# New orders for a fused DeltaNet and Fourier-mix kernel: a plan in which loads in flight delay instruction packets

## The chip, the cores and the metric

The kernel runs on one core of a Trainium2 chip. Its time is the device time of one execution in microseconds (us); the median of the runs is compared. Engines are named as in the profile: PE is TensorE's matrix multiply and PEld its weight load, DVE is VectorE, ACT is ScalarE, POOL is GpSimd, SP is the engine that issues most loads and stores.

## The reference

Two blocks stand one behind the other, all in 32-bit floats. The first is a DeltaNet recurrence over 768 positions for 4 batches of 8 heads with 48 channels; the second mixes positions and channels by a Fourier transform, normalises each row, and applies a two-layer MLP.

```python
for t in range(S):
    y[:, :, t] = np.einsum('bhd,bhde->bhe', q[:, :, t], state)
    v_old = np.einsum('bhde,bhd->bhe', state, kt)
    state = state + bt[:, :, :, None] * np.einsum('bhd,bhe->bhde', kt, vt - v_old)
...
X = np.fft.fft(x, axis=1)                      # x is y as (batch, position, 384)
X = np.fft.fft(X, axis=2)
u = x + np.real(X)
un = (u - mean(u)) / np.sqrt(var(u) + 1e-06)
out = u + np.maximum(un @ w_ch1, 0.0) @ w_ch2   # 384 -> 1536 -> 384
```

`kt` is `k` divided by its norm, `bt` the factor beta.

## The kernel before

The recurrence is done in chunks. A unit is 128 positions of one batch with all 8 heads; there are 24 units, six for each batch. For each unit the kernel loads keys, queries and values, turns keys and queries with transposes on TensorE (`turn`), forms products of keys with keys and of queries with keys (`keys`, `gram`), and inverts a triangular matrix of 32x32 blocks for all its heads. The inversion is a long chain of small products and sums on VectorE. Units are inverted in rounds: four and two units for batch 0 (`begin16`, `invert16` in blocks of 16, put together by `join` with matmuls of `gd` and `w2` or `w1`), then three units for each round (`begin`, `invert`). After that the state runs through the units one half (64 positions) at a time: `chain0`, `values0` and `outputs0` for batch 0, `step` and `outputs` for the others. The tiles `us0` to `us5` hold a unit's keys, queries and values; a later unit takes the tile of an earlier one when that is done.

When a batch is complete, `mixing` does its second block: `folds` uses the symmetries of the Fourier transform on VectorE, `seq` multiplies by the table `tab` along positions, `half_axis` copies the result out of PSUM (`g0`) and mirrors it (`g2`), `feat` multiplies by `ft` along channels, `normed` normalises and transposes, and `mlp` or `mlpw` does the MLP. The MLP's matmuls are the bulk of TensorE's time; those of one batch fill TensorE while VectorE inverts for the next. The weights are loaded in pieces and recoded at the start by ScalarE, VectorE and GpSimd (`weights`), with stages in tiles that are used for something else later (`ws`, `x1`, `R0`, `R1`).

Nothing of the order is written out by hand. Each operation is recorded by `Plan.op` with its engines and estimated durations, what it reads and writes, its PSUM banks and a priority. `Plan.schedule` then runs through an imitated time: each engine takes, when it is free, the ready operation with the least `pr`, which comes from the due times, the priority and a small pseudo-random shift (`shift`, by `KEYS`, one key for each 64 operations). The instructions are given out in that order, and on the chip each engine works through its own list in order and waits by semaphores for data alone: the imitated times are not on the chip.

The plan imitates several things of the chip. `speed` imitates TensorE's clock by its load in windows of `WIN` us, at half speed when cold. `fetch` imitates the packets in which TensorE's instructions come, one for each `BLOCK` of 256 instructions; an operation can't end before its packet has come. `bursts` are the stretches in which loads are in flight; with `HOLDUP` at 0.0, they delay no packet before the change. `moved` is the time at which the loads so far have landed, at `RATE` KB per us.

Where TensorE has nothing to do and its load would fall below a target, the plan puts in a filler (`idle`): matmuls on `pb` or `pack` into a free bank, whose result nobody reads. A filler is six matmuls of 64 columns in the first 5 us of the plan, later one of 256 columns on 128 rows or two on 64 rows each. The opening, from the first load to the first matmul of `join`, thus consists of transposes and products of keys with fillers between them.

Two small things are also touched. `half` holds the 1e-6 under the roots: `pads` zeroes it, then `eps` sets it on GpSimd; the first square root on ScalarE reads it, and a load of ScalarE's function table comes with that. Two long memsets of `w2` and `w1` and one of `bcol` stand on GpSimd at the start as well. And in `half_axis`, `g0` copies a PSUM row that holds the positions in `m` groups into one in which they alternate.

Of the kernel before, what the change touches and what calls it, by code (L numbers as in the profile page):

```python
# [21 lines left out]
KEYS = [0, 0, 850, 0, 0, 0, 0, 0, 0, 0, 0, 0, 582, 124, 156, 527, 24, 416, 593, 575, 248, 102, 531, 777, 887, 940, 929, 917, 359, 0, 859, 298, 364, 930, 55, 217, 906, 105, 134, 603, 98, 513, 101, 281, 683, 240, 529, 252]  # L22
# [10 lines left out]
class Op:  # L33
# [4 lines left out]
RATE = 190.0  # L38
WIN, WARM, COLD, CLOCK = 3.413, 600.0, 560.0, True
LOOK, EARLY = 1e9, 19.0271  # L40
FOLD, BY, SEQ, HOT, HOTPE, HOTPK, HOTG, NORM = 1, 1, 1, 4.4058, 0, 0, 0, 1
HOTC, PORT, E2 = 2, 1, 5.0
GAP, HALF = 0.2407, 77.3251
LATE = 2.2375
PLOOK, PHOLD, PEND = 32.7105, 0.4568, 120.0484
NHALF = 1
FORCE = 612.9049
BLOCK, LEAD, SEEK, LAND, LAND2, HOLDUP = 256, 60, 1.0, 2.4, 2.0082, 0.0
# [8 lines left out]
M00 = 90.055  # L57
M0, MP, MX, MN, MA, MT, MD = 89.6079, 112.2722, 14.7505, 25.9652, 19.5299, 4.5034, 5.8147


LATER = {"SHARE": 0.3855, "HOLD": 0.1688, "GAP2": 0.3021, "WAIT": 10.3631, "GATHER": 2.1078, "URGENT": -9.2156,
         "FIRST": 59.6475, "EV": 2.2994, "STAY": 0.4162, "CHAIN": 1.0}
START = {"SHARE": -0.1525, "HOLD": 0.3422, "GAP2": 0.0341, "WAIT": 8.3074, "GATHER": 1.5733, "URGENT": -10.6776,
         "FIRST": -0.9418, "EV": 10.7255, "STAY": 0.0, "CHAIN": 0.0}
LIM2 = {"state": 1, "sum": 4, "attn": 7, "mix": 5, "mlp": 6, "norm": 7, "win": 6}
# [6 lines left out]
class Plan:  # L72
# [114 lines left out]
    def schedule(self, pick, limits, switch, idle=None, span=()):  # L187
# [18 lines left out]
        moved, landed = 0.0, [0.0] * 8  # L206
# [12 lines left out]
        while done < n:  # L219
# [4 lines left out]
            for e in self.ENG:  # L224
# [3 lines left out]
                cand = [o for o in avail[e] if o.ready[e] <= now + 1e-9]  # L228
                if e != "PE":
# [72 lines left out]
                o = best  # L302
# [11 lines left out]
                if o.kb:  # L314
# [3 lines left out]
                    self.bursts.append((moved - o.kb / RATE + 1.0, moved + 0.7))  # L318
                    self.bursts = self.bursts[-6:]
# [34 lines left out]
            if not progressed:  # L354
# [3 lines left out]
                nxt += [s for s in slots if s is not None and s > now + 1e-9]  # L358
                nxt += [b.busy for e in ("DVE", "ACT") for o in avail[e] for b in o.banks
# [75 lines left out]
def kernel(  # L435
# [135 lines left out]
    def psum(b):  # L571
        return pst[b.slot]
# [951 lines left out]
    def half_axis(bk, gs, m, sn, pr):  # L1524
# [503 lines left out]
    P.op({"POOL": 0.3}, eps, [], [A(half, 0, 1)], -60, lat=LP)  # L2028
# [240 lines left out]
```

## Time and profile before

| | before |
|---|---|
| median of 3 runs | 646.76 us (646.76 to 652.67) |
| the profiled execution | 651.29 us, span 649.5 us |
| TensorE busy | 627.6 us (97%) |
| VectorE busy | 512.0 us (79%) |
| ScalarE busy | 268.3 us (41%) |
| GpSimd busy | 35.4 us (5%) |
| bytes moved | 32.01 MB, mean 49 GB/s |

The span goes from the first to the last instruction of the profiled execution; the rest of its time lies around it. A group of instructions is given by the line of the kernel that issues it. Helpers issue most of them: 533 is every matmul (`mm`), 536 every transpose on TensorE (`tr`), 542 a copy on ScalarE, 544 and 546 a copy on VectorE (`copy`), 580 a load (`dma`), 2224 and 2231 the fillers. A matmul shows as two records. The granted clock is the share of TensorE's full clock that the chip let through.

### The profile page before, as it was taken

To read this page: it belongs to the slowest core of one execution; us is meant where nothing else is said; L and a number is where in the kernel's file an instruction comes from. 1 tells how busy PE (TensorE), PEld (TensorE's weight loads), DVE (VectorE), ACT (ScalarE), POOL (GpSimd) and SP (SyncE) were. 2 spreads that over 40 slices of the span, in tenths; PEclk is the share of its full clock that TensorE was granted. 3 is DMA by queue.
4 is the path that set the end of the run, shared out by engine and by line. 5 is a ranking of instruction groups with operands and counts; after the bars stand their busy time and mean duration, and the time that the engine had idled before them with its cause. 6 is when DMAs were issued, how large, how long until landed. Compare 5 with 4: busy or idle time off the path is not lost.

```text
span 649.5 us, 23061 instructions
## 1 busy us (share of the span) xinstructions
PE 627.6 (97%) x9958; PEld 517.9 (80%) x9958; DVE 512.0 (79%) x1533; ACT 268.3 (41%) x784; POOL 35.4 (5%) x40
## 2 busy tenths in 40 slices
PE   8898989999999999999999999999999999999998
PEld 7698878876767777877777877777777789999997
DVE  5979959999996469999973899999838724986573
ACT  4768554652126544521645551435452113321120
POOL 3001212221000000000000000000000000000000
PEclk9989979999999999999999999999999999999999
DMA  9912456430003312000232310000000000000000
GB/s 189 283 76 45 97 124 150 110 106 2 24 3 88 77 40 51 25 2 1 52 63 53 65 50 2 1 26 3 4 28 3 1 25 1 26 1 25 2 25 24
DMA packets 82810, 32.01 MB, mean 49 GB/s; under 512 B 75667, under 2 KB 79732, under 8 KB 82580
## 3 DMA queue, kind: packets, MB, share of 16 engines
q1 hardware_dynamic: 82516, 30.31, 19.0%
q8 instruction: 78, 1.28, 0.8%
q10 hardware_dynamic: 192, 0.23, 0.1%
q14 instruction: 24, 0.20, 0.1%
HBM read 25.81 MB, written 4.72 MB: 47 GB/s over the span
## 4 chain that ended last, share of the span: by engine, by line
PE 75%; DVE 18%; issue 3%; ACT 3%; DMA 1%; SPq 0%; DVEq 0%; ACTq 0%
PE pp L533 70%; PE pp L2231 3%; PE pp L536 2%; DVE rr L1018 2%; DVE tmp L1013 2%; DVE R L1418 1%; DVE pm L1596 1%; DMA ws<-in_moe_w_ch_dram 1%; PE pp L2224 1%; ACT us L542 1%; DVE w L2001 1%; ACT R L542 1%; DVE x L1578 1%; DVE rr L820 1%; DVE us L782 1%
## 5 line engine op out<-in xcount | busy, mean ns | idle before, releaser
L533 PE MATMUL pp<-R,w 128*128 128x256 f32 (+1 forms) x832 | 182.2, 367 | 0.5 <-DVE x L1393 0.3
L533 PEld LDWEIGHTS pp<-R,w 128*128 128x128 f32 x832 | 145.9, 190 | 20.2 <-DVE x L1393 0.5
L533 PE MATMUL pp<-w,R 128*128 128x384 f32 x384 | 136.4, 499 | 0.9 <-DVE w L2001 0.9
L533 PEld LDWEIGHTS pp<-w,R 128*128 128x128 f32 x384 | 71.1, 192 | 43.2 <-issue 2.0
L542 ACT ACTIVATE us<-pp 32x128 f32<-32x128 f32 (+3 forms) x232 | 73.0, 349 | 72.0 <-PE pp L533 51.7
L533 PE MATMUL pp<-us 64*64 64x64 f32 (+4 forms) x2784 | 67.7, 230 | 7.1 <-issue 5.6
L1662 ACT ACTIVATE R<-pp 128x512 f32<-128x512 f32 x48 | 28.6, 596 | 98.5 <-PE pp L533 93.8
L533 PEld LDWEIGHTS pp<-us 64*64 64x64 f32 (+2 forms) x2784 | 57.1, 133 | 13.0 <-issue 9.1
L1018 DVE TENSOR_TENSOR rr<-rr,tmp 128x30 f32<-128x30 f32 (+14 forms) x180 | 55.7, 330 | 0.8
L1013 DVE TENSOR_TENSOR tmp<-rr 128x30 f32<-128x30 f32 (+14 forms) x180 | 55.0, 326 | 0.8
L533 PEld LDWEIGHTS pp<-u,us 64*64 64x64 f32 (+1 forms) x1472 | 36.9, 132 | 16.4 <-issue 10.4
L533 PE MATMUL pp<-u,us 64*48 64x48 f32 (+2 forms) x1472 | 43.2, 220 | 1.9 <-DVE u L544 0.7
L1327 DVE TENSOR_TENSOR u<-u,pp 64x192 f32<-64x192 f32 x66 | 21.9, 350 | 19.8 <-PE pp L533 17.1
L542 ACT ACTIVATE R<-pp 128x192 f32<-128x192 f32 (+7 forms) x76 | 25.0, 384 | 28.0 <-PE pp L536 14.1
L1837 DVE TENSOR_TENSOR us<-us,pp 128x256 f32<-128x256 f32 x64 | 26.8, 419 | 12.0 <-ACT us L542 10.2
L542 ACT ACTIVATE x<-pp 64x192 f32<-64x192 f32 (+1 forms) x80 | 24.4, 323 | 25.3 <-PE pp L533 22.6
L1356 DVE TENSOR_TENSOR st<-st,pp 128x192 f32<-128x192 f32 x30 | 10.5, 351 | 28.3 <-PE pp L533 28.2
L1793 DVE TENSOR_TENSOR gd<-us 128x128 f32<-128x128 f32 x48 | 11.9, 287 | 24.2 <-ACT us L1869 17.0
L542 ACT ACTIVATE u<-pp 64x192 f32<-64x192 f32 (+1 forms) x71 | 23.0, 326 | 17.9 <-PE pp L533 13.6
L2231 PE MATMUL pp<-pack 64*64 64x256 f32 (+1 forms) x170 | 29.0, 408 | 0.4 <-ACT R L542 0.4
L533 PE MATMUL pp<-st,us 48*64 48x48 f32 (+1 forms) x1232 | 27.9, 223 | 1.2 <-ACT us L542 0.9
L533 PEld LDWEIGHTS pp<-st,us 48*64 48x64 f32 x1232 | 23.8, 136 | 5.3 <-issue 3.7
(172 smaller groups left out, 997.0 us busy)
## 6 DMA issues: line engine op xcount, KB each, us to landing
out_dram<-x SPq DMA_DIRECT2D x11, 384.0 KB
us<-in_k_dram SPq DMA_DIRECT2D x16, 192.0 KB
us<-in_q_dram SPq DMA_DIRECT2D x16, 192.0 KB
us<-in_v_dram SPq DMA_DIRECT2D x16, 192.0 KB
us<-in_v_dram SPq DMA_DIRECT2D x8, 181.5 KB
us<-in_q_dram SPq DMA_DIRECT2D x8, 181.5 KB
us<-in_k_dram SPq DMA_DIRECT2D x8, 181.5 KB
x<-in_moe_w_ch_dram SPq DMA_DIRECT2D x3, 484.0 KB
```

The lines of the kernel that those rows point to most:

```text
L533: I(nc.tensor.matmul(o, lhsT=lhsT, rhs=rhs, start=start, stop=stop, skip_group_check=True))
L536: I(nc.tensor.matmul(o, lhsT=src, rhs=ident[p0:p0 + n, p0:p0 + n], is_transpose=True, start=start, stop=True, skip_group_check=True))
L542: I(nc.scalar.activation(o, i, ACT.Copy, **({} if scale is None else {"scale": scale})))
L782: I(eng(e).tensor_tensor(z.V, z.V, ro.nr(160 + 8 * ul, 8)[:, :, None].broadcast_to([128, H, D]), op=ALU.mult))
L1013: I(eng(e).tensor_tensor(T_, R[:, :, j + 1:32, j:j + 1].broadcast_to([128, ns, n, j]), R[:, :, j:j + 1, 0:j].broadcast_to([128, ns, n, j]) ...
L1018: I(eng(e).tensor_tensor(R[:, :, j + 1:32, 0:j], R[:, :, j + 1:32, 0:j], T_, op=ALU.add))
L1327: I(nc.vector.tensor_tensor(U[:, s], U[:, s], psum(b1[s])[a, s0:s1].rearrange("p (j d) -> p j d", d=D), op=ALU.subtract))
L1356: I(nc.vector.tensor_tensor(sn[:, s0:s1], so[:, s0:s1], psum(b2)[:, s0:s1], op=ALU.add))
L1662: I(nc.scalar.activation(o, s, ACT.Relu))
L1793: vec(128, lambda e, j=j, i0=i0, i1=i1, op=op: I(nc.vector.tensor_tensor(s(j), i0, i1, op=op)), [aH] + rd, [aS(j)], pr - P.ev)
L1837: vec(256, lambda e: I(nc.vector.tensor_tensor(o, i0(), i1(), op=ALU.add)), [], [aH] + list(wr), pr - P.ev, use=n)
L2231: I(nc.tensor.matmul(pst[two[0]][x, 0:256], lhsT=w[x, 0:n], rhs=w[x, 0:256], start=True, stop=True, skip_group_check=True))
```

## The change

The change has three kinds of edits.

First, the plan imitates more. `crowd` gives the share of the stretch from 0.5 us before to 1.5 us after a time in which loads are in flight, and `fetch` delays a packet by `HOLDUP`, now 1.8 us, times that share. The list of bursts is longer, and each ends 0.3 us later. `moved` begins at `MOVED`, 1.6 us, instead of 0, so that all loads land later in the plan. Between `PACE` and `PEND` of imitated time, SP gets no load until the loads before have moved (`PGAP`).

Second, nearly all constants of the plan and a good half of the `KEYS` are new, so the order of all engines is new from the first operations on.

Third, two operations are edited: `eps` has the priority -460 instead of -60, and `g0` runs through its row in the order of the destination, where it ran in the order of the source.

```diff
-KEYS = [0, 0, 850, 0, 0, 0, 0, 0, 0, 0, 0, 0, 582, 124, ...]
+KEYS = [555, 372, 229, 658, 0, 352, 821, 0, 0, 291, 803, 38, 709, 968, ...]
...
-LATE = 2.2375
-PLOOK, PHOLD, PEND = 32.7105, 0.4568, 120.0484
+LATE = -8.0806
+PLOOK, PHOLD, PEND = 28.9494, 0.7158, 110.1635
 NHALF = 1
-FORCE = 612.9049
-BLOCK, LEAD, SEEK, LAND, LAND2, HOLDUP = 256, 60, 1.0, 2.4, 2.0082, 0.0
+FORCE = 613.4279
+BLOCK, LEAD, SEEK, LAND, LAND2, HOLDUP = 256, 60, 1.0, 2.401, 1.9048, 1.8
+PACE, PGAP, MOVED = 4.1415, -0.0594, 1.6
...
-TARGET, SPANW = 688.3225, 2.1272
-E0, E1, D1 = 1.0, 10.0, 128.0771
-TSW = 114.3489
-LIM = {"state": 1, "sum": 3, "attn": 7, "mix": 4, "mlp": 5, "norm": 2, "win": 4}
-NW, IV, IV1, WP = 9, 13.8489, 26.4887, -10.2966
+TARGET, SPANW = 685.5687, 2.0943
+E0, E1, D1 = 1.0, 10.0, 105.9979
+TSW = 108.6907
+LIM = {"state": 1, "sum": 3, "attn": 7, "mix": 6, "mlp": 8, "norm": 2, "win": 4}
+NW, IV, IV1, WP = 9, 14.9091, 10.2325, -10.5791
...
+    def crowd(self, t):
+
+        return min(1.0, sum(max(0.0, min(z, t + 1.5) - max(a, t - 0.5)) for a, z in self.bursts) / 2.0)
...
-            for a, z in self.bursts:
-                if a <= t < z:
-                    t = min(z, t + HOLDUP)
-                    break
+            t += HOLDUP * self.crowd(t)
...
-        moved, landed = 0.0, [0.0] * 8
+        moved, landed = MOVED, [0.0] * 8
...
+                if e == "SP" and PACE < now < PEND:
+                    cand = [o for o in cand if not o.kb or moved + PGAP <= now + 1e-9]
...
-                    self.bursts.append((moved - o.kb / RATE + 1.0, moved + 0.7))
-                    self.bursts = self.bursts[-6:]
+                    self.bursts.append((moved - o.kb / RATE + 1.0, moved + 1.0))
+                    self.bursts = self.bursts[-12:]
...
-                o = Fv[0:n, g, 0:hs].rearrange("p (k a) -> p a k", a=m)
-                copy(e, o, psum(bk[g % 2])[0:n, 0:m * w].rearrange("p (a k) -> p a k",
-                                                                   a=m)[:, :, 0:w - 1])
+                o = Fv[0:n, g, 0:hs].rearrange("p (k a) -> p k a", a=m)
+                copy(e, o, psum(bk[g % 2])[0:n, 0:m * w].rearrange("p (a k) -> p k a",
+                                                                   a=m)[:, 0:w - 1])
...
-    P.op({"POOL": 0.3}, eps, [], [A(half, 0, 1)], -60, lat=LP)
+    P.op({"POOL": 0.3}, eps, [], [A(half, 0, 1)], -460, lat=LP)
```

More of the change, by code (lines that the diff above doesn't have):

```diff
@@ L40 @@
 LOOK, EARLY = 1e9, 19.0271
-FOLD, BY, SEQ, HOT, HOTPE, HOTPK, HOTG, NORM = 1, 1, 1, 4.4058, 0, 0, 0, 1
-HOTC, PORT, E2 = 2, 1, 5.0
-GAP, HALF = 0.2407, 77.3251
-LATE = 2.2375
-PLOOK, PHOLD, PEND = 32.7105, 0.4568, 120.0484
+FOLD, BY, SEQ, HOT, HOTPE, HOTPK, HOTG, NORM = 1, 1, 1, 2.0724, 0, 0, 0, 1
+HOTC, PORT, E2 = 1, 1, 5.0
+GAP, HALF = 0.3228, 84.1105
+LATE = -8.0806
+PLOOK, PHOLD, PEND = 28.9494, 0.7158, 110.1635
 NHALF = 1
-FORCE = 612.9049
-BLOCK, LEAD, SEEK, LAND, LAND2, HOLDUP = 256, 60, 1.0, 2.4, 2.0082, 0.0
+FORCE = 613.4279
+BLOCK, LEAD, SEEK, LAND, LAND2, HOLDUP = 256, 60, 1.0, 2.401, 1.9048, 1.8
+PACE, PGAP, MOVED = 4.1415, -0.0594, 1.6
 CUT, ROW = 512, 121
@@ L51 @@
 WF = 2, 2
-TARGET, SPANW = 688.3225, 2.1272
-E0, E1, D1 = 1.0, 10.0, 128.0771
-TSW = 114.3489
-LIM = {"state": 1, "sum": 3, "attn": 7, "mix": 4, "mlp": 5, "norm": 2, "win": 4}
-NW, IV, IV1, WP = 9, 13.8489, 26.4887, -10.2966
[L57 to L65, printed above, removed]
+TARGET, SPANW = 685.5687, 2.0943
[3 more added lines that the diff above has]
+NW, IV, IV1, WP = 9, 14.9091, 10.2325, -10.5791
+M00 = 102.6459
+M0, MP, MX, MN, MA, MT, MD = 89.6079, 112.293, 14.26, 39.3785, 20.7101, 5.6373, 6.1497
+LATER = {"SHARE": 0.3909, "HOLD": 0.1688, "GAP2": 0.3179, "WAIT": 10.0453, "GATHER": 2.2916, "URGENT": -9.2156,
+         "FIRST": 60.1548, "EV": -0.0518, "STAY": 0.4103, "CHAIN": 1.0}
+START = {"SHARE": -0.1569, "HOLD": 0.3422, "GAP2": 0.1697, "WAIT": 5.8104, "GATHER": 1.3282, "URGENT": -10.6776,
+         "FIRST": 2.0404, "EV": 10.4613, "STAY": 0.0, "CHAIN": 0.0}
+LIM2 = {"state": 1, "sum": 4, "attn": 7, "mix": 6, "mlp": 7, "norm": 7, "win": 6}
 T_F3, T_F2, T_PAIR = 0.36, 0.32, 0.52
@@ L358, in schedule @@
                 nxt += [s for s in slots if s is not None and s > now + 1e-9]
+                if avail["SP"] and PACE < now < PEND and moved + PGAP > now + 1e-9:
+                    nxt.append(moved + PGAP)
                 nxt += [b.busy for e in ("DVE", "ACT") for o in avail[e] for b in o.banks
```

2 lines of the change are left out of this document (1 added, 1 removed).

## The prediction

> **What bounds the kernel now.** I read the page first: the busy shares, then the 40 slices.
>
> ```profile
> span 649.5 us, 23061 instructions
> PE 627.6 (97%) x9958; PEld 517.9 (80%) x9958; DVE 512.0 (79%) x1533; ACT 268.3 (41%) x784; POOL 35.4 (5%) x40
> ...
> PEclk9989979999999999999999999999999999999999
> ```
>
> TensorE is busy 97% of the span. Since the change orders the same arithmetic anew, I asked next where TensorE is not full, or not at full clock: stretches with the busy time of each engine (us from:to, length, then PE, PEld, DVE, ACT, POOL, then granted clock, DMA share and GB/s).
>
> ```profile
> 0.00:40.00 40.00, 35.32 (x666) 29.79 (x667) 29.91 (x132) 22.09 (x63) 7.65 (x16) 0.96 0.83 221
> 40.00:80.00 40.00, 37.55 (x1330) 35.44 (x1328) 34.97 (x85) 29.64 (x92) 8.01 (x7) 1.00 0.25 53
> 80.00:92.00 12.00, 8.66 (x230) 8.18 (x228) 5.60 (x16) 5.92 (x19) 2.57 (x2) 0.72 0.52 115
> ...
> 120.00:200.00 80.00, 75.52 (x691) 54.95 (x692) 79.59 (x227) 27.51 (x75) 10.41 (x9) 1.00 0.17 44
> ...
> 320.00:330.00 10.00, 8.94 (x213) 6.06 (x200) 7.23 (x26) 5.63 (x20) 0.00 (x0) 0.83 0.20 39
> 330.00:640.00 310.00, 309.39 (x4215) 260.32 (x4214) 225.92 (x669) 107.36 (x310) 0.31 (x1) 1.00 0.08 21
> ```
>
> From 330 to 640 us TensorE misses 0.6 us in 310: no order can win there. From 120 to 200 VectorE is the full engine (79.59 of 80). What can be won lies before 120 us, in four places: the opening, the fillers (matmuls on `pack` or `pb` whose results nobody reads, put in by `idle`), the waits of TensorE, and the low clock. The group of the fillers and the longest of TensorE's waits:
>
> ```profile
> L2231 PE MATMUL pp<-pack 64*64 64x256 f32 (+1 forms) x170 | 29.0, 408 | 0.4 <-ACT R L542 0.4
> ```
>
> ```profile
> PE pp L533 <- issue: 7.5, 7, 2.9
> ```
>
> "issue" is a wait for nothing the profile shows: neither a semaphore nor data. The longest, with its place (timeline of TensorE):
>
> ```profile
> 83.61 0.94 PE L533 MATMUL pp<-us 48*64 48x128 f32 x22 [2.94 <-issue]
> ```
>
> TensorE stands 2.94 us while loads run (115 GB/s in 80 to 92). In that stretch the mean clock is 0.72, which costs 12 x 0.28 = 3.4 us more; 320 to 330 at 0.83 costs 1.7. The new plan is about stalls of this kind.
>
> **The opening.** TensorE's instructions in order of time (start, us; the bracket is the idle time before):
>
> ```profile
> 1.18 5.09 PE L2224 MATMUL pp<-pb 128*64 128x64 f32 x48 [1.18 <-DVE pb L655]
> ...
> 7.08 1.56 PE L2231 MATMUL pp<-pb 128*128 128x256 f32 x6
> 8.57 0.71 PE L536 MATMUL pp<-pack,us 64*128 64x64 f32 x16
> ...
> 13.14 0.40 PE L536 MATMUL pp<-pack,us 64*128 64x64 f32 x6 [1.07 <-issue]
> 13.47 1.13 PE L2231 MATMUL pp<-pack 128*128 128x256 f32 x4
> ...
> 14.92 0.70 PE L2231 MATMUL pp<-pack 128*128 128x256 f32 x2
> ...
> 16.53 6.21 PE L2231 MATMUL pp<-pack 64*64 64x256 f32 x56
> ```
>
> ```profile
> 32.14 0.28 PE L533 MATMUL pp<-us 48*64 48x64 f32 x3 [2.22 <-issue]
> ...
> 32.31 7.89 PE L2231 MATMUL pp<-pack 64*64 64x256 f32 x55
> 39.94 1.27 PE L533 MATMUL pp<-gd,w 64*64 64x64 f32 x36
> ```
>
> ```profile
> 34.94 1.05 DVE L948 STREAM_TRANSPOSE gd<-w 128x512 f32<-128x512 f32 x1
> ```
>
> The matmul at 39.94 is the first of `join`; it reads what the transpose wrote by 35.99, so TensorE comes 3.95 us late, because its queue of fillers is not done. So TensorE's own queue sets the opening, and VectorE's chain is the floor below it. An instruction shows as two records. In the built order of the changed kernel the opening differs so: 42 instead of 24 small fillers (line 2224) ahead of the first data; 2 instead of 6 of 128x256 up to the sixth key tile; 30 instead of 28 of 64x256 behind it; 2 instead of 3 of 128x256 after that; the last 28 stay. Priced: 18 x 2 = 36 records at 5.09 / 48 = 0.106 us is 3.8 us at most; at the rate of the neighbouring 64x64 records (0.71 / 16 = 0.044) it is 1.6. I take 2.0, near the low end, for they stand where those neighbours run. The 128x256 ones fall from 1.56 + 1.13 + 0.70 = 3.4 to two of 0.70: -2.0. Two of 64x256 at 6.21 / 28 = 0.22: +0.4. One of 128x256 at 1.13 / 2: -0.6. Together -0.2. It could be -3.95 (the floor of VectorE) or +1.6 (the high price); the two stalls, 1.07 and 2.22, I leave as they are.
>
> **The memset of the table load.** The change gives `eps` an earlier priority, -460. Yet POOL's order is the same in both kernels: `pb`, `gd`, the 4352 columns of `w2`, `eps`.
>
> ```profile
> 1.44 3.73 POOL L2131 MEMSET w<- 128x4352 f32 x1
> 5.11 0.10 POOL L2027 MEMSET eps<- 128x1 f32 x1
> ```
>
> ```profile
> 1.64 0.06 DVE L655 MEMSET eps<- 128x1 f32 x1
> ```
>
> ```profile
> 7.10 1.28 ACT L2029 ACT_TABLE_LOAD   x1
> ```
>
> `eps` overwrites what VectorE zeroes at 1.64, and POOL starts the long one at 1.44: that part does not do what it says, and costs nothing. The table load still stands among the copies of the first key tiles, now behind two of `us0` instead of one (VectorE's copy went to ScalarE); the 0.3 us that this adds for the next tile lies under the fillers.
>
> **The loads.** On SP the value loads of the first units go between the query loads, so the last query load is issued behind four more.
>
> ```profile
> 5.74 6.56 SPq L580 DMA_DIRECT2D us<-in_q_dram  x6
> ```
>
> ```profile
> 27.79 0.46 PE L536 MATMUL pp<-pack,us 64*128 64x64 f32 x8
> ```
>
> One takes 6.56 / 6 = 1.1 us to issue, so the last goes out near 12.3 + 4.4 = 16.7 instead of 12.3; its first reader starts at 27.79: covered by 11 us, and 4.4 us if that cover were gone. From the second set of units on, queries and keys stand ahead of values, and the pieces of weights move up some five to ten places. In the queue each waits for its buffer, and what is behind it waits too; the first is now a query, whose buffer `outputs0` frees, not a value. Values are needed last, so I cost this at 0 and leave the collision with instruction packets to a rival. `PACE` holds SP back in the plan alone: no instruction waits on it on the chip.
>
> **The chain of batch 0 and its mixing (40 to 120 us).** TensorE's real instructions are the same 5134, and batch 0's chain ends after the same 926 behind the first join; modes change 189 times instead of 192. What falls is the fillers: 4 instead of 10 of 64x256 in the chain, 3 instead of 6 of 128x256 in the mixing. By the prices above that is 6 x 0.22 = 1.3 and 3 x 0.56 = 1.7. A filler stands where TensorE would wait otherwise, so the gain is between 0 (the wait stays) and 3.0; I take 2.2, since the plan found real work for most of these places. Later fillers: five against five, and two at the end in both.
>
> **The stall at 80.67.** The plan counts one packet for 256 instructions (`BLOCK`), and the same work stands there. The new order puts the second weight pieces closer behind the first, so the burst is no shorter. I take 0 here, between -2.94 - 3.4 = -6.3 (gone, with its low clock) and +6.3 (a second one like it).
>
> [...]
>
> **The copy out of the sequence transform.** `g0` now writes its row in order and reads PSUM in strides.
>
> ```profile
> 266.37 1.57 ACT L542 ACTIVATE R<-pp 96x384 f32<-96x384 f32 x2 [4.86 <-PE pp L533]
> 267.72 0.94 ACT L542 ACTIVATE R<-R 96x383 f32<-96x383 f32 x2
> ```
>
> The strided write takes 0.79 each against 0.47 for a copy of the same length with an ordered write. Three batches have four each; two engines share some, and MLP matmuls cover most. If all stood on the path: 12 x 0.32 = -3.8; if strided reading is as dear as strided writing, 0; dearer by as much, +3.8. I take -0.5: a tenth or so is uncovered.
>
> **The sum.** -0.2 + 0 + 0 - 2.2 + 0 - 0.5 = -2.9 us. The profiled execution took 651.29 us (span 649.5 and 1.8 around it): 648.4 for one like it. The median of the runs shown is 646.76, 4.5 lower; the 3.4 + 1.7 = 5.1 us of low clock are the nearest thing in the profile to that difference, and since I change nothing there, the same step off the median gives 646.76 - 2.9 = 643.9 us.
>
> **The rivals.**
> - *More is won than fillers.* TensorE reaches the join when the transpose is done (-3.9 instead of -0.2), and the copy comes out cheaper by another 1.5: 643.9 - 3.7 - 1.5 = 638.7. For it: 3.95 us of lateness is there to be had, and after 120 VectorE sets the pace, so an earlier opening is carried through. Against: the same 28 fillers stand ahead of the join.
> - *Slower: packets meet loads in the chain.* SP does not know the plan's pacing, so loads leave as soon as buffers are free; the weights that moved up fall together with queries and keys on a packet in 55 to 85 us, TensorE stands another 2.94 us and runs 3.4 us' worth at low clock; the longer burst of small fillers at the high price delays the opening by 1.6 more, and the fillers' 2.2 are lost in the wait: 643.9 + 6.3 + 1.6 + 2.2 = 654.0. It decides once over 2.9 us of stall is added. For it: three such stalls stand in the trace, all during loads. Against: the chain's stretch 40 to 80 moves only 53 GB/s.
> [...]
>
> **The numbers.** Forecast (643.9) 0.36, more (638.7) 0.28, slower (654.0) 0.25, no difference (646.8) 0.11. About 1%, 6.5 us, is what a measurement of this kernel can tell from no change: faster below 640.3, slower above 653.2. The forecast's own range is 640 to 646.5 (its unknowns in the opening and the fillers); a little of it lies below 640.3, and part of the slower case stays under 653.2. So faster by over 1% 0.31, within 1% 0.48, slower 0.21. The range for 8 in 10 reaches into both outer cases: 637 to 654.
>
> **What would show it.** Right: the first `us0` transpose starts near 8.2 instead of 6.2, the join near 39.8; the 64x256 and 128x256 fillers after the join fall from 23 to 14 and TensorE's idle time in 40 to 120 does not grow; `g0` near 0.5 us; POOL's order unchanged. Wrong: the join before 37 or after 42 us; an "issue" wait over 2 us in 40 to 80 or none at all in 40 to 120; a stretch of low clock that before did not have, or the loss of the one at 80 to 92; a stretch after 200 us that takes another time than before.

## The result, and the profile after

| | before | after |
|---|---|---|
| median, us | 648.62 (17 runs, 646.76 to 653.51) | 654.69 (17 runs, 649.59 to 658.24) |
| profiled execution, us | 651.29 (span 649.5, clock 0.989) | 654.0 (span 652.2, clock 0.986) |

The ratio is 1.0076, with an interval of 1.005 to 1.0101: the change makes the kernel about 5 us slower. The forecast was 643.9. The range's upper end, 654, and the rival "slower" at 654.0 lie next to what was measured, but the cause turned out to be another than the rival's. The forecast started from a median of 646.76 in three runs; 17 runs put before at 648.62, so 1.9 of the 10.8 us between 643.9 and 654.69 is the starting point and not the change.

The page of the kernel after, its totals and its clock:

```profile
span 652.2 us, 23088 instructions
...
PE 625.3 (96%) x9970; PEld 515.1 (79%) x9970; DVE 513.3 (79%) x1538; ACT 265.5 (41%) x779; POOL 35.0 (5%) x40
...
PEclk9998889899999999999999999999999999999999
```

The same stretches as the prediction showed, now of after (us from:to, length, busy time of PE, PEld, DVE, ACT, POOL, granted clock, DMA share, GB/s), with 200 to 230 added:

```profile
0.00:40.00 40.00, 36.09 (x752) 28.74 (x754) 29.05 (x129) 20.76 (x63) 7.65 (x16) 1.00 0.83 221
40.00:80.00 40.00, 33.32 (x1133) 31.69 (x1127) 34.97 (x88) 28.45 (x83) 8.29 (x8) 0.91 0.26 56
80.00:92.00 12.00, 10.01 (x324) 9.61 (x326) 7.27 (x18) 6.33 (x16) 3.59 (x3) 0.86 0.31 73
120.00:200.00 80.00, 75.21 (x640) 54.22 (x642) 78.74 (x226) 28.37 (x76) 10.93 (x9) 0.98 0.23 57
200.00:230.00 30.00, 27.12 (x996) 22.86 (x992) 14.14 (x39) 19.33 (x63) 0.00 (x0) 0.94 0.39 83
320.00:330.00 10.00, 10.00 (x214) 7.66 (x206) 9.25 (x29) 6.42 (x22) 0.00 (x0) 1.00 0.43 103
330.00:640.00 310.00, 309.60 (x4171) 259.67 (x4170) 224.46 (x666) 103.49 (x304) 0.31 (x1) 1.00 0.07 19
```

The row of before that was not shown yet:

```profile
200.00:230.00 30.00, 29.55 (x965) 24.01 (x963) 12.80 (x35) 18.41 (x59) 0.00 (x0) 1.00 0.39 83
```

Two stretches lose. From 40 to 80 TensorE is busy 33.32 us instead of 37.55 and its clock falls from 1.00 to 0.91: 4.2 us of waits and 40 x 0.09 = 3.6 us of clock. Some 1.3 us of these waits are only moved: a wait that both kernels have begins at 78.74 in after and at 80.67 in before, and so it counts to the next row in before. Over 40 to 120 us together (before, then after)

```profile
40.00:120.00 80.00, 73.41 (x2024) 67.73 (x2022) 67.02 (x175) 51.79 (x155) 16.71 (x13) 0.96 0.42 96
40.00:120.00 80.00, 69.53 (x1916) 65.14 (x1910) 68.45 (x183) 51.06 (x146) 15.81 (x13) 0.94 0.36 83
```

TensorE's idle time grows from 6.6 to 10.5 us, and there are three stretches of low clock instead of two. From 200 to 230 TensorE is busy 27.12 instead of 29.55, and its clock is 0.94 instead of 1.00: 2.4 and 1.8. At 80 to 92 after is 3.0 better, in part by the moved wait, and at 320 to 330 it is 2.8 better; 120 to 200 costs 1.9. After 330 both are full.

TensorE's longest waits in after, and the first matmuls of its opening:

```profile
PE pp L539 <- issue: 10.1, 10, 2.8
PE pp L539 <- DVE st L550: 2.1, 1, 2.1
PE pp L539 <- DVE t L1052: 1.9, 1, 1.9
PE pp L542 <- DVE pm L1602: 1.4, 1, 1.4
```

```profile
1.18 7.53 PE L2230 MATMUL pp<-pb 128*64 128x64 f32 x84 [1.18 <-DVE pb L661]
8.64 0.46 PE L542 MATMUL pp<-pack,us 64*128 64x64 f32 x8
...
38.33 2.03 PE L539 MATMUL pp<-gd,w 64*64 64x64 f32 x64
```

The join starts at 38.33 instead of 39.94. This is clock and not order: from 0 to 40 us before ran at 0.96, with one stretch of low clock from 33.1 to 36.5, and after at 1.00. Which of the two after's opening gets changes from one execution to the next. Of the eleven profiles with after's opening, those of the experiments included, six have such a stretch, and their joins start at 38.60 to 40.34. In the eight with before's opening, all with the stretch, it is 38.95 to 40.56. The kernel after, profiled once more (after_again below), has

```profile
39.13 2.03 PE L867 MATMUL pp<-gd,w 64*64 64x64 f32 x64
```

Whether after's opening is spared the stretch more often than before's is not settled. The chain gains on top: up to 62 us TensorE is some 4 us ahead of before: it starts the first matmuls of a state (`st,R`) at 53.9, 59.2 and 62.1, where before starts its at 57.9, 63.1 and 66.9. The next one starts at 70.4 in after and at 70.5 in before. So the whole lead goes between 62 and 70 us: from the third state to the fourth it is 8.3 us in after and 3.7 in before. This repeats: in the five other profiles that have after's order of TensorE, VectorE and ScalarE there (after_again, a_loads_b, w_cut_a, open_before, chain_after) it is 8.2 to 8.4. This is the place (timelines of TensorE, VectorE, GpSimd and ScalarE there; for VectorE, `L772` is the multiply of a unit's table by its mask and `L550` its copies):

```profile
67.77 0.45 PE L539 MATMUL pp<-u,us 64*64 64x64 f32 x8 [1.13 <-issue]
70.36 0.68 PE L539 MATMUL pp<-st,R 48*64 48x64 f32 x16 [2.15 <-DVE st L550]
```

```profile
64.96 0.76 DVE L1999 TENSOR_SCALAR w<-w 128x512 int32<-128x512 int32 x2
65.63 3.47 DVE L772 TENSOR_TENSOR us<-us,pack 128x512 f32<-128x512 f32 x2
69.03 0.41 DVE L1991 TENSOR_SCALAR w<-w 128x512 f32<-128x512 f32 x1
69.36 0.68 DVE L772 TENSOR_TENSOR us<-us,pack 128x512 f32<-128x512 f32 x1
69.96 0.34 DVE L550 COPY st<-pp 128x192 f32<-128x192 f32 x1
```

```profile
65.52 1.35 POOL L2004 TENSOR_TENSOR w<-w,ws 128x512 int32<-128x512 int32 x1 [5.94 <-issue]
66.82 1.74 POOL L2004 TENSOR_TENSOR w<-w,x 128x512 int32<-128x512 int32 x1
```

```profile
68.26 0.33 ACT L548 ACTIVATE x<-pp 128x192 f32<-128x192 f32 x1 [2.07 <-PE pp L539]
71.07 0.32 ACT L548 ACTIVATE u<-pp 64x192 f32<-64x192 f32 x1 [2.48 <-PE pp L539]
```

TensorE waits 2.15 us for the copy of a state. In after that copy stands on VectorE behind three table multiplies and a recode of weights. Two of the multiplies take 3.47 us together, 1.7 each, where the third takes 0.68: GpSimd adds two tiles (L2004) beside the two, and nothing beside the third. None of the three is needed at once: tt_late below moves them behind, 1 to 5 us later. ScalarE stands idle for 2.07 and 2.48 us there. In before the same copy runs on ScalarE.

### The profile page after: what moved, and what is told of

The parts are those of the page before. It is cut to its first block, busy times and chain, and to the rows that moved or that the text cites. A ratio compares the mean times of both kernels' runs of the same rounds, so it can differ in the third digit from the quotient of the medians.

```text
span 652.2 us, 23088 instructions
## 1 busy us (share of the span) xinstructions
PE 625.3 (96%) x9970; PEld 515.1 (79%) x9970; DVE 513.3 (79%) x1538; ACT 265.5 (41%) x779; POOL 35.0 (5%) x40
## 4 chain that ended last, share of the span: by engine, by line
PE 76%; DVE 17%; ACT 3%; issue 3%; DVEq 0%; ACTq 0%
PE pp L539 70%; PE pp L2237 3%; PE pp L542 3%; DVE tmp L1019 2%; DVE rr L1024 2%; ACT us L548 1%; DVE rr L826 1%; PE pp L2230 1%; DVE R L1424 1%; DVE gd L780 1%; DVE w L2007 1%; DVE eo L1424 1%; DVE pm L1424 1%; DVE pm L1602 1%; DVE x L1399 0%
## 5 line engine op out<-in xcount | busy, mean ns | idle before, releaser
L539 PE MATMUL pp<-R,w 128*128 128x256 f32 (+1 forms) x832 | 184.6, 370 | 0.7 <-ACT R L548 0.4
L539 PEld LDWEIGHTS pp<-R,w 128*128 128x128 f32 x832 | 146.8, 192 | 20.4 <-issue 1.0
L539 PE MATMUL pp<-w,R 128*128 128x384 f32 x384 | 134.9, 494 | 1.1 <-DVE w L2007 1.1
L539 PEld LDWEIGHTS pp<-w,R 128*128 128x128 f32 x384 | 70.3, 190 | 42.6 <-DVE w L2007 1.7
L539 PE MATMUL pp<-us 64*64 64x64 f32 (+4 forms) x2784 | 70.3, 232 | 7.1 <-issue 5.7
L539 PEld LDWEIGHTS pp<-us 64*64 64x64 f32 (+2 forms) x2784 | 59.2, 133 | 13.5 <-issue 9.4
L1024 DVE TENSOR_TENSOR rr<-rr,tmp 128x198 f32<-128x198 f32 (+14 forms) x180 | 54.3, 322 | 0.9
L1019 DVE TENSOR_TENSOR tmp<-rr 128x198 f32<-128x198 f32 (+14 forms) x180 | 54.1, 320 | 0.8
L539 PEld LDWEIGHTS pp<-u,us 64*64 64x64 f32 (+1 forms) x1472 | 38.5, 134 | 18.7 <-issue 13.8
L539 PE MATMUL pp<-u,us 64*48 64x48 f32 (+2 forms) x1472 | 45.0, 221 | 3.5 <-issue 2.4
L1362 DVE TENSOR_TENSOR st<-st,pp 128x192 f32<-128x192 f32 x30 | 10.6, 352 | 36.7 <-PE pp L539 36.5
L548 ACT ACTIVATE R<-pp 128x192 f32<-128x192 f32 (+7 forms) x79 | 22.4, 330 | 37.7 <-PE pp L539 20.8
L539 PE MATMUL pp<-st,us 48*64 48x48 f32 (+1 forms) x1232 | 29.0, 223 | 1.0 <-ACT u L548 0.7
L539 PEld LDWEIGHTS pp<-st,us 48*64 48x64 f32 x1232 | 24.6, 136 | 4.4 <-issue 2.9
L1399 DVE TENSOR_TENSOR x<-x,pp 64x192 f32<-64x192 f32 x66 | 23.3, 352 | 5.8 <-PE pp L539 3.9
L539 PE MATMUL pp<-us,gd 128*128 128x192 f32 x144 | 27.5, 326 | 0.0
```

The costliest lines, as they stand in the source:

```text
L539: I(nc.tensor.matmul(o, lhsT=lhsT, rhs=rhs, start=start, stop=stop, skip_group_check=True))
L548: I(nc.scalar.activation(o, i, ACT.Copy, **({} if scale is None else {"scale": scale})))
L1019: I(eng(e).tensor_tensor(T_, R[:, :, j + 1:32, j:j + 1].broadcast_to([128, ns, n, j]), R[:, :, j:j + 1, 0:j].broadcast_to([128, ns, n, j]) ...
L1024: I(eng(e).tensor_tensor(R[:, :, j + 1:32, 0:j], R[:, :, j + 1:32, 0:j], T_, op=ALU.add))
L1362: I(nc.vector.tensor_tensor(sn[:, s0:s1], so[:, s0:s1], psum(b2)[:, s0:s1], op=ALU.add))
L1399: I(nc.vector.tensor_tensor(w, w, v, op=ALU.add))
```

## The experiments

Each comparison ran the kernel before beside it, so every ratio has a before of its own. "Order up to X" means that the instructions of all engines are issued in that kernel's recorded order up to X and in the other's from there. A kernel with a written-out order has its line numbers some 330 higher (L862 and L867 are the matmul of L533 and L539). One more reading goes through them all. The runs carry the granted clock, so I split each mean time into time x clock (what it would be at full clock, if a stretch at 0.5 loses half its length) and the rest (what low clock costs):

| kernel | ratio to before | interval | full clock + low clock, us | before beside it |
|---|---|---|---|---|
| open_after | 1.0033 | 1.0003 to 1.0062 | 645.3 + 4.5 | 642.8 + 4.5 |
| open_before | 1.0118 | 1.0081 to 1.0155 | 648.2 + 7.4 | the same |
| chain_after | 1.0084 | 1.005 to 1.0118 | 643.4 + 9.1 | the same |
| chain_before | 1.007 | 1.0047 to 1.0093 | 646.0 + 6.2 | the same |
| g0_only | 1.0017 | 0.9988 to 1.0046 | 643.4 + 4.7 | 642.3 + 4.1 |
| st_act | 1.0041 | 1.0012 to 1.0069 | 642.8 + 6.7 | the same |
| b_st_dve | 1.0037 | 1.0006 to 1.0068 | 644.9 + 4.7 | the same |
| a_loads_b | 1.024 | 1.0208 to 1.0272 | 651.0 + 13.0 | the same |
| w_cut_b | 0.9933 | 0.9908 to 0.9958 | 643.2 + 2.2 | 644.0 + 6.1 |
| w_cut_a | 1.0094 | 1.0063 to 1.0124 | 644.8 + 10.8 | the same |
| tt_late | 1.0018 | 0.9985 to 1.0051 | 643.0 + 8.1 | the same |
| b_w_late | 1.0025 | 0.9999 to 1.0051 | 645.5 + 5.8 | the same |
| after_again | 1.0145 | 1.0091 to 1.02 | 643.9 + 13.2 | 643.5 + 4.8 |
| tt_late_cut | 1.0046 | 1.0014 to 1.0078 | 642.3 + 8.4 | the same |
| tt_rest_b | 1.0029 | 0.9993 to 1.0065 | 642.8 + 7.5 | the same |
| b_w_k | 0.9993 | 0.9965 to 1.0021 | 643.8 + 3.7 | the same |
| after_fill | 1.0101 | 1.0049 to 1.0153 | 647.1 + 8.0 | 643.7 + 4.8 |
| tt_fill | 1.0056 | 1.0018 to 1.0094 | 645.9 + 6.0 | the same |

The 17 runs of after in the first comparison split into 644.8 + 9.2. The most telling row is after_again: on one chip, after is 0.4 us slower than before at full clock and 8.3 us slower by its clock. It warns as well: the same order of instructions gave 1.0076 in one comparison and 1.0145, with six runs, in another. Ratios of different comparisons that lie closer than that tell little.

**Where along the run: four splices.** The join is the first matmul of the chain of batch 0; the other border is the first matmul of the MLP.

> The order of the changed kernel up to the first join matmul, from there the order of the kernel before, with its copy g0. Theory 1 (the loss is made in the chain of batch 0, after the join): 1.6 us faster than before, since the join came at 38.33 instead of 39.94. Rival A (the longer opening itself costs the loss): about 5 us slower. Rival B (the loss is made after 125 us): 1.6 us faster, as in theory 1.

> The order of the kernel before up to the first join matmul, from there that of the changed kernel, with its copy g0. Theory 1: 6.5 us slower than before (the loss of 5 without the 1.6 won in the opening). Rival A: no difference. Rival B: 6.5 us slower, as in theory 1.

> The order of the changed kernel up to the first MLP matmul of batch 0 (opening, chain and transform of batch 0), from there the order of the kernel before. Theory 1: the whole loss, about 5 us slower than before. Rival A: the same. Rival B: 0 to 1.6 us faster.

> The order of the kernel before up to the first MLP matmul of batch 0, from there that of the changed kernel, with its copy g0. Theory 1: no difference to before. Rival A: no difference. Rival B: about 5 us slower.

Opening and chain of after with the rest of before (chain_after) cost as much as the whole change, and before's opening with the rest of after costs more (open_before, 1.0118, 7.6 us where Theory 1 expected 6.5): Theory 1 holds so far. But the rest of after alone (chain_before) costs 1.007 too, and the parts do not add up to 1.0076, nor does the opening win anything by itself (open_after, 1.0033). A splice joins two orders that were not made for each other, so it tells where to look, not how much is there.

**The copy g0 alone.**

```diff
-                o = Fv[0:n, g, 0:hs].rearrange("p (k a) -> p a k", a=m)
+                o = Fv[0:n, g, 0:hs].rearrange("p (k a) -> p k a", a=m)
```

(and the same turn on the side of PSUM; nothing else.)

> The kernel before, instruction for instruction in the same order, with only the copy g0 written the new way. In the profile after, the copy of 96x384 took 0.48 us instead of 0.87. Theory (the copy lies almost all beside other work): 0 to -1.0 us, a ratio of 0.998 to 1.000. Rival (the copies stand on the path: 12 of them by 0.39): -4.6 us, a ratio of 0.993. A ratio over 1.002 would make the copy itself the cause of the loss.

1.0017, no difference. The copy itself is cheaper: the group by shape went from

```profile
L542 ACT ACTIVATE R<-pp 96x384 f32<-96x384 f32 x5 | 4.3, 869 | 7.5 <-PE pp L533 7.5
```

in before to

```profile
L548 ACT ACTIVATE R<-pp 96x384 f32<-96x384 f32 x6 | 2.9, 482 | 10.5 <-PE pp L539 10.4
```

in after, 869 to 482 ns, but the interval of g0_only leaves at most 0.8 us of gain: the 4.6 us of the rival are ruled out.

**VectorE's queue ahead of the state: one copy, both ways.** st_act moves it off VectorE in after; b_st_dve puts it there in before.

```diff
 DVE, st_act:
 L1100 TensorTensor us_80<-us_80,pack 128x512
-L878 TensorCopy st_92<-pp_62 128x192
 ACT, st_act:
+L876 Activation st_92<-pp_62 128x192
```

> The kernel after with one instruction on another engine: the copy of the state (st, 128x192), which TensorE waits 2.15 us for at 70.36, goes to ScalarE (which runs it in the kernel before, and stands idle there) instead of standing on VectorE behind three table multiplies (line 772) that take 1.78 us instead of 0.68 while GpSimd multiplies. Theory 2 (this queue is where the chain of after loses): the wait at 70.36 falls below 0.5 us and the low clock behind it goes, -2.2 to -3.9 us against after, a ratio to the kernel before of 1.002 to 1.004. Rival (the time is only passed on: the next fetch or the next state waits instead): a ratio of 1.006 to 1.008, as after.

> The mirror image: the kernel before with the same copy of the state put on VectorE behind the same three table multiplies and the one recode between them; nothing else is moved, TensorE's order is that of before. Theory 2: TensorE waits about 2 us for st, perhaps with a window of low clock, +2.2 to +3.9 us, a ratio of 1.003 to 1.006. Rival (such a wait is made good later): 1.000 to 1.002.

In b_st_dve, TensorE's order being that of before, the wait appears where Theory 2 puts it,

```profile
72.22 1.07 PE L862 MATMUL pp<-st,R 48*64 48x64 f32 x16 [2.70 <-DVE st L873]
```

with a stretch of low clock from 72.3, and the ratio is 1.0037, +2.4 us. (In this profile the wait called issue near 80 us is not there, so 2.4 us may be what is left of one wait that came and one that went.) In st_act the wait for the state is gone, and the fourth state comes 4.2 us after the third; but the next copy behind the same multiplies is late in its place, and so 1.0041 is only part of the way back:

```profile
69.73 0.47 PE L867 MATMUL pp<-u,us 64*64 64x64 f32 x9 [2.51 <-DVE u L878]
```

**The multiplies moved instead.**

```diff
 DVE:
-L1100 TensorTensor us_79<-us_79,pack 128x512
-L1100 TensorTensor us_77<-us_77,pack 128x512
 L2319 TensorScalarPtr w_73<-w_73 128x512
-L1100 TensorTensor us_80<-us_80,pack 128x512
 L878 TensorCopy st_92<-pp_62 128x192
 L878 TensorCopy x_96<-pp_63 128x4x48
 L878 TensorCopy u_85<-pp_61 64x4x48
+L1100 TensorTensor us_79<-us_79,pack 128x512
 ...
```

> The kernel after with three of VectorE's instructions moved: the table multiplies (line 772, 128x512) that stand ahead of the copies of state, x and u at 69.96 to 71.12 go behind them, one by one, 1 to 5 us later; all else as in after. Theory 2 (VectorE's queue in front of the state copy): the wait of 2.15 us at 70.36 falls below 0.5, and the 2.5 us wait for u that took its place when only the state copy was moved is not there either; -2 to -4 us against after, a ratio to before of 1.001 to 1.004. Rival (passed on): 1.006 to 1.008.

1.0018: with three instructions of 23,088 moved by 1 to 5 us, the ratio falls from 1.0076 to 1.0018, each against the before beside it, which would be 3.8 of 4.9 us; the two intervals just touch (1.005 and 1.0051). From the third state to the fourth it is 5.3 us instead of 8.3. The wait is down to

```profile
68.16 0.68 PE L867 MATMUL pp<-st,R 48*64 48x64 f32 x16 [0.94 <-DVE st L878]
```

At this place Theory 2 stands. The rival "passed on" is true of a part: at 75.39 TensorE now waits 1.42 us for another copy, behind the last of the three.

The 3.8 us are not the price of this queue alone. In the profile of tt_late the wait called issue near 79 us is gone too: no wait of this kind from 70 to 95 us is over 0.5, though all weights are loaded, and the packet of instructions that starts at 77.82 is in time (250 records, in the count that follows). It is the same in st_act, tt_rest_b and tt_fill. Moving VectorE's work also moved the packet away from the loads.

**Loads and packets.** The DMA records of the trace show the packets of instructions for TensorE (in before 78 of 16 KB, queue q8 on its page, for 2 x 9958 records of matmuls and weight loads, 255 each), and how many records of the block before had started when each packet did. From 50 to 105 us most start at 190 to 310 (178 of 241 in all twenty profiles). The late ones, and the same packet in four other kernels:

```
kernel     packet starts   records of the block before        wait called issue next to it
before          80.64                 421                        2.94 from 80.67
after           78.98                 426                        2.84 from 78.74
w_cut_b         77.99                 288                        none over 0.65
w_cut_a         78.71                 248                        none over 0.65
b_w_k           78.93                 290                        none over 0.65
tt_late         77.82                 250                        none over 0.65
```

> The kernel after with SyncE issuing its loads and stores in the order of the kernel before; the order on the four other engines is that of after. The prediction's rival (loads moved by the new plan meet instruction packets in the chain): the waits that the profile calls issue at 67.77 and 81.58 (1.13 and 2.84 us) and in 205 to 230 us go or shrink, the ratio to before falls to 1.000 to 1.003. Theories 1 and 2 (the order of the work on VectorE and ScalarE): the ratio stays at 1.006 to 1.009.

> The kernel before, every engine in its order, but two pieces of weights (ws and x, issued at 76.28 and 77.27 in the profile before) bring only 14 of their 128 rows; the other rows keep older weights, so this leaves out part of the load. Why: packets of instructions for TensorE start when 190 to 310 records of the block before have been done, but the one at 80.64 starts at 421, 3 to 4 us after these loads were issued, and TensorE then waits 2.94 us. Theory F (the bulk of the weights holds the packet up): no packet between 70 and 90 us starts above 330 records, the wait called issue there falls below 1 us, -1.6 to -4 us, a ratio of 0.993 to 0.998. Rival (the packet is late for another reason, or the wait is passed on to the next one): 0.999 to 1.002.

> The same cut of two pieces of weights (14 of 128 rows; the rest keeps older weights) in the kernel after, where they are issued at 72.10 and 74.25 and the packet at 78.98 starts at 426 records, with a wait of 2.84 us. Theory F: that wait falls below 1 us, -1.6 to -4 us against after, a ratio to before of 1.001 to 1.005. Rival: 1.006 to 1.009, as after. If both cuts gain alike, this wait is no part of the difference between the two kernels.

> The kernel before, whole, with two pieces of weights issued by SyncE behind the four loads of keys and queries that followed them; all else as before. Theory F: the packet leaves ahead of the weights, the wait called issue near 80.67 shrinks, -1 to -3 us, a ratio of 0.995 to 0.999. Rival: the weights only fall on the next packet, or come late for their recode: 1.000 to 1.005.

In w_cut_b and w_cut_a the kernel leaves out 114 of the 128 rows of two loads of weights. The cut bears out Theory F for before: with the bulk of the weights gone the packet is in time, the wait is gone, and so is the low clock (76 to 92 us, w_cut_b first, then before):

```profile
76.00:92.00 16.00, 14.53 (x498) 12.98 (x495) 13.32 (x37) 11.02 (x33) 3.96 (x3) 1.00 0.53 114
```

```profile
76.00:92.00 16.00, 12.66 (x373) 11.98 (x370) 9.42 (x25) 8.07 (x24) 3.93 (x3) 0.79 0.54 123
```

It is worth 4.4 us of the whole time, 3.9 of them clock (6.1 to 2.2). At full clock it wins only 0.8, though the wait in the profile was 2.94. In after the packet is in time too, but the ratio is 1.0094, no better than after's. TensorE stands 3.89 us for the state:

```profile
71.62 1.12 PE L867 MATMUL pp<-st,R 48*64 48x64 f32 x16 [3.89 <-DVE st L878]
```

The cut did not make this wait longer: the cut loads are issued at 73.80, behind it, and from the third state to the fourth it is 8.2 us as in after. So the late packet, the matter the new plan is about, does not make the difference of the two kernels: without it in either, after is 1.6% slower than before (1.0094 / 0.9933, one comparison), twice the whole change. How long it is changes by execution or order (1.61 us in g0_only, whose order is before's; 2.17 in after_again; 4.08 in chain_before). B_w_late shows what else the loads decide: its packet is in time (286 records), but at 87.55 TensorE waits 2.76 us for ScalarE, and the ratio is 1.0025. The order of loads is not the cause either: SyncE's order of before under the rest of after is far worse (a_loads_b, 1.024; TensorE waits 3.9 and 3.2 us for states and 3.8 for a load of keys). The new order of loads suits the new order of work, against the prediction's rival.

**Together, and a whole kernel.**

> The kernel after once more, its order written out, as an anchor on the same chip for the three others: a ratio to before of 1.005 to 1.010 by the first comparison.

> The kernel after with the three table multiplies moved behind the state copy and with the two pieces of weights cut to 14 of 128 rows (the rest keeps older weights). Alone these gave a ratio to before of 1.0018 and 1.0094. Theory 3 (the two waits lie over one another: in after VectorE's queue holds the chain up even when the packet is in time): together they gain more than the sum, a ratio of 0.992 to 0.999. Rival (the cut does nothing in this order): 1.000 to 1.003, as the moved multiplies alone.

> A whole kernel: up to the first matmul of the MLP the order of after with the three table multiplies moved, then the order of before, with the new copy g0. Without the move this splice was 1.0084. If the queue of VectorE was the whole loss, and the rest of after costs something (Rival B, 2 to 4 us by the splices): 0.996 to 1.001. If the rest costs nothing: 1.001 to 1.004. If a splice as such costs: above 1.004.

> A whole kernel: before with the two pieces of weights issued by SyncE behind the two loads of keys that followed them (not behind those of queries, where the weights came too late and ScalarE held TensorE up for 2.76 us). Theory F: the packet near 78 starts at 250 to 330 records as in the cut kernel, the wait near 80.67 falls below 1.5 us and nothing comes late: 0.994 to 0.999. Rival (the next packet meets the weights instead): 0.999 to 1.004.

After_again came out slower than the anchor I expected (1.0145). Tt_late_cut gives 1.0046: the two gains do not add, and Theory 3 is wrong. The reason is in the profiles: with the multiplies moved the packet is in time already, and the cut has nothing to take away. With neither wait, then, this order still takes 1.0018 (tt_late) to 1.0046 of before's time, where before without its packet wait takes 0.9933: by these ratios, and as far as one profile of each tells, the queue is a third to a half of what after loses on this footing (1.0094 down to 1.0046 or 1.0018, of 1.0094 down to 0.9933). The rest is not found. Tt_rest_b, 1.0029, is neither below before nor clearly above tt_late's 1.0018: what the rest of after loses between 200 and 230 us is seen in the busy time (below) but not in the median. B_w_k, 0.9993, has its packet in time, and then waits 1.73 us for ScalarE at 86.40, which waits for the later weights: the gain of the cut is not to be had by this order. No kernel that loads everything came out clearly faster than before.

**Filling the waits.** If the clock is the cost, matmuls that nobody reads should win in the waits what they cost.

```diff
 PE, after_fill (five more such places):
+Matmult pp<-pack 64x256 x10
 Matmult pp<-st,R 64x64
```

> The kernel after, every engine in its order, with 14 more fillers (matmuls on pack that nobody reads) on TensorE, each group right ahead of an instruction that waits on VectorE or ScalarE: 2 at 51.6, 2 at 53.6, 5 at 70.4 (64x256, 0.2 us each and less than the waits of 0.9, 0.8 and 2.2), then of 128x256 (0.6 each) 2 at 121.9, 1 at 157.4 and 2 at 188.2 (waits of 1.4, 1.1, 1.9). Theory 4 (after loses by its clock: more waits that leave TensorE busy for less than about 0.6 of a 3.4 us stretch, each of which makes the next stretch run at 0.5): 2 to 4 low stretches fewer, the part at full clock unchanged within 1 us, a ratio to before of 1.000 to 1.006. Rival (the clock is only a companion of lost time; a filler is more work): 1.008 to 1.015.

> The kernel after with the three table multiplies moved behind the copies (the last of them one place further, behind the copy of 128x512 that TensorE waited 1.42 us for) and 12 fillers ahead of the same instructions (2 ahead of the state's). A whole kernel. Theory 4: both gains together, a ratio to before of 0.994 to 1.000; rival: 1.002 to 1.006, as with the moved multiplies alone.

The fillers did their part: in the profile of after_fill no stretch of low clock starts between 35 and 92 us, nor from 97 to 205 us, where after and after_again have them near 54, 70, 82, 122 and 190. But the ratio is 1.0101. What low clock costs fell from 9.2 (or 13.2) to 8.0 us, and what full clock costs rose from 644.8 (643.9) to 647.1. New waits stand elsewhere, of the kind called issue:

```profile
90.42 0.66 PE L875 MATMUL pp<-us 48*64 48x128 f32 x15 [2.07 <-issue]
...
209.20 0.26 PE L875 MATMUL pp<-us 64*32 64x32 f32 x1 [1.91 <-issue]
...
220.75 0.33 PE L875 MATMUL pp<-us 64*64 64x48 f32 x8 [1.56 <-issue]
```

The packet ahead of the first started at 404 records. So Theory 4 holds for the clock at the filled places and fails for the time. Tt_fill, with the multiplies moved as well, gives 1.0056, in its rival's range.

**The second place, 200 to 230 us.** The same row for kernels with the rest of after (tt_late, chain_before) and with that of before (tt_rest_b, b_w_k):

```profile
200.00:230.00 30.00, 26.37 (x915) 21.94 (x914) 14.02 (x39) 19.70 (x63) 0.00 (x0) 1.00 0.36 70
```

```profile
200.00:230.00 30.00, 26.96 (x1053) 23.15 (x1048) 13.05 (x37) 20.21 (x66) 0.00 (x0) 1.00 0.38 83
```

```profile
200.00:230.00 30.00, 28.05 (x897) 22.06 (x894) 9.99 (x29) 16.74 (x54) 0.00 (x0) 0.94 0.35 69
```

```profile
200.00:230.00 30.00, 29.27 (x973) 23.75 (x973) 10.98 (x31) 18.15 (x58) 0.00 (x0) 0.99 0.36 70
```

In all twenty profiles it is so: TensorE is busy 25.3 to 27.7 us with the rest of after and 28.0 to 29.9 with the rest of before. The waits in it are "issue" (1.51, 0.43 and 0.77 us at 209.69, 221.41 and 225.35 in after), while queries and keys of the next units load. Over 200 to 330 us TensorE is 1.8 us less busy in after than in before (125.44 against 127.19), at the same mean clock of 0.99.

## Why the prediction was wrong

- **The chain's fillers, -2.2, is the step that failed.** The fillers did fall: their group, x170 and 29.0 us before, is in after

```profile
L2237 PE MATMUL pp<-pack 64*64 64x256 f32 (+1 forms) x150 | 22.0, 381 | 1.0 <-DVE us L757 1.0
```

  But "the plan found real work for most of these places" was not so. The prediction's own test decides: TensorE's idle time in 40 to 120 was not to grow, and it grew from 6.6 to 10.5 us, by 3.9, while the fillers there fell from 6.1 to 3.0 us: waits took their place, and more. I had bounded the term by 0, "the wait stays". That was the wrong bound: the order that took the fillers out also put a state copy behind three multiplies on VectorE, and a new wait can be longer than the filler that it replaces. From the third state to the fourth it took 4.6 us more (8.3 against 3.7). The order of VectorE's instructions was there to be compared, and I had compared TensorE's and GpSimd's.
- **The low clock, taken as unchanged, is the larger part.** "Since I change nothing there" was the error: low clock kept to no place, and most of it stood behind waits (50 of 60 beginnings behind a TensorE that was busy for at most 0.60 of 3.4 us, counted below). After has 9.2 and 13.2 us of it, before 4.1 to 6.1. Of the 5 us, some 3 to 5 are clock, and 8 in after_again.
- **After 200 us the prediction expected no difference**, and said that another time there would prove it wrong. It did: 2.4 us less busy in 200 to 230, 1.8 in 200 to 330. In the medians this cost is not separated from the rest.
- **The opening, -0.2 (between -3.95 and +1.6),** fits: the joins at 38.60 to 40.34 with after's opening and 38.95 to 40.56 with before's, all at a clock of 0.96, differ by no more. The 1.6 us of this profile are the stretch of low clock that its opening was spared; after_again, the same order, was not, so they are luck. The first `us0` transpose starts at 8.64 (8.2 forecast). The lead of 4 us at 62 us shows that "more" was possible, up to the state copy; after_again has it too, at 62.16, with its join at 39.13.
- **Memset 0 and the stall at 80.67 0 were right**: GpSimd's order is unchanged, and the stall is 2.84 us instead of 2.94 in these two profiles. That the same order can show it shorter (1.61 in g0_only, 2.17 in after_again) is not in the prediction. The loads at 0 were right as to the packets; that the new order of work needs them (1.024 without) I had not seen.
- **The copy, -0.5:** its price was right (0.48 forecast as "near 0.5"), its effect is none that can be measured (g0_only).
- **The rival "slower" had the size and not the mechanism.** It wanted loads to hold packets up for another 2.94 us in the chain. The packet waits grew little there (2.94 us in before; 1.13 and 2.84 in after, and the 1.13 cost nothing, for without them too the fourth state comes 8.2 us after the third); what it lacked was VectorE's queue. Its clock term, 3.4 us, was of the right size. No difference (646.8) is refuted by the result (1.005 to 1.0101) and by b_st_dve (1.0006 to 1.0068), which moves four of VectorE's instructions and one copy, and changes nothing that is computed.

What stays open: why the order of before is 2 us slower behind the opening of after (open_after, 1.0033); and the larger part of what after loses on equal footing, for with neither the state's wait nor the late packet it is still 0.8 to 1.1% slower than before without that packet (1.0018 and 1.0046 against 0.9933). The waits in 200 to 230 us are the nearest thing to it, and tt_rest_b, which has before's order there, did not come out faster. A version of after with all three kinds of wait removed was not found.

## What to carry to other kernels

When a reordering takes fillers or slack out of the busiest engine's queue, compare the order on the engines that feed it, and look for work that is not urgent ahead of a copy that it waits for; here one such place cost a lead of 4 us. Price a wait on TensorE by itself and by the clock that may go behind it (here stretches of 3.4 us at 0.5), and look at more than one profile before a difference of one such stretch, 1.7 us, is put down to the order. Take out the wait, not its symptom: filling it held the clock here and cost as much (after_fill, 1.0101).

## What the runs showed of the hardware that was not expected

**A wait of 1.4 us can cost 1.7 more.** Low clock comes in stretches of 3.4 us at 0.5 (in before one from 33.1 to 36.5, two in a row from 84.3 and one from 323.2; in after from 54.3, 71.4, 81.6, 122.6 and 211.3). Over all twenty profiles, 60 of them begin behind a stretch of full clock; in 50 of these TensorE was busy for at most 0.60 of the 3.4 us before, and only 13 stretches as little busy were not followed by one. In after TensorE was busy for 1.26 of the 3.41 us before 71.4. So waits that sum to 1.4 us (0.4 of 3.4) in the 3.4 us before were mostly enough. The price is an estimate, half of 3.4 us; in before 20 records of the fillers stand in 33.10 to 36.51, at 0.50, and 36 in 36.52 to 40.00, at 1.00. The executions of one kernel differ by it: the 17 of after run from 649.59 at a mean clock of 0.992 to 658.24 at 0.977.

**VectorE's multiply of two SBUF operands takes 1.7 instead of 0.68 us while GpSimd adds two tiles** (rows at 65.63, 65.52 and 66.82 above; L2004 is an addition of integers, not the multiplication that the expectation of st_act names). Of the twelve multiplies of this line in before and after, the three beside such an addition take 1.76 to 1.79 us, two of them in after and the one at 70.36 in before; the nine others take 0.65 to 0.68. The queue behind the multiply pays for it: in after the state copy starts at 69.96, and TensorE waits 2.15 us for it.

**A packet of instructions starts late behind a burst of loads**: at 421 records in before, and at 288 once two loads of weights were cut to 14 of their 128 rows (w_cut_b). The prediction had read the three stalls so, and for this one the cut bears it out in before's order. As far as these runs show, it is the burst close ahead of the packet that delays it, not the burst as such: with all rows loaded the packet starts at 290 records where two loads of keys go ahead of the weights (b_w_k), and at 250 in tt_late, where the weights are issued at 70.50 to 72.07, 6 us ahead of the packet, instead of 72.10 to 74.90, 4 us ahead, in after.
